# Block-causal attention feeding a feed-forward on one Trainium2 core: another order of a pair's eight steps from batch 2 on

## The chip, the cores and the metric

The kernel runs on one core of a Trainium2 chip. The metric is device time in microseconds, the median of several executions; less is better. Five engines work side by side, each through a queue of its own: TensorE (PE, with its weight loads PEld), VectorE (DVE), ScalarE (ACT), GpSimd (POOL), and SyncE (SP), which issues every DMA of this kernel.

## The reference

Attention in 8 batches of 8 heads, 576 positions, 64 elements a head; a position sees its own block of 64 positions and all earlier blocks. The heads' outputs, side by side, are the 4608 x 512 input of a feed-forward of width 2048.

```
scores = q @ k.T / sqrt(64)
scores = where(pos_i // 64 >= pos_j // 64, scores, -1e9)
attn   = exp(scores - max) / (sum + 1e-9)
x      = (attn @ v), heads side by side         # 4608 x 512
h      = x @ w_in                               # 4608 x 2048
g      = 0 where h <= -1, h where h >= 1, else (h + 1)^2 / 4
out    = g @ w_out                              # 4608 x 512
```

## The kernel before, in words

**Pairs and steps.** The work goes by pairs of heads: 8 batches of 4 pairs, 32 in all. `attention_steps` is a generator that emits a pair's attention in eight steps, each ended by a `yield` (L688, L699, L711, L722, L733, L742, L750, L759). From the 36th step on (`START`, L830) the main loop puts one half of a feed-forward tile behind each step: `ffn_in` (12 matmuls of 512 columns into the bank `ph`, then ScalarE `t`, two VectorE operations L780 and L783, ScalarE `gh`, GpSimd `gl`) or `ffn_out` (12 matmuls into `po`, for the tile before the last). In the pairs spoken of here, `ffn_out` stands behind steps 1, 3, 5 and 7, and `ffn_in` behind 2, 4, 6 and 8. What is left of the feed-forward runs alone at the end.

**Three kinds of pairs.** Pairs of batches 0 and 1 run in ways of their own. From batch 2 on (`FAR`, `RAW` = 2) a pair is "far": each operand is split into a high and a low part in float32r; a pair's last transpositions and its products with v reach into the next pair's steps. `cur` is the pair whose scores are made, `old` the one before, `nxt` the one after.

**What a far pair does.** For each head j there are three groups of query tiles (`GROUPS`, L258 on): group 0 (score tiles of 128 and 256 columns), group 1 (384) and group 2 (512); the last 64-position blocks of both heads make one further group, "last".
- `scores(j, g)` (L494): two matmuls a tile into a work bank; VectorE maximum (L505); ScalarE exponential with its sum (L509); VectorE adds the epsilon (L491), inverts (L492) and scales (L515) `pr`. Then a DMA copies `pr` to a float32r tile `prr` (`as_float32r`, L230, issued at L250). `scores_last` (L518) does this in two banks of 288 columns.
- `turn(j, g)` (L556): three or four transpositions of `prr` into a work bank (L552); ScalarE casts the high part (L545), VectorE subtracts it for the low part (L547). Group 0 goes to `pa`, groups 1 and 2 to `pb`. `turn_last` (L572) does four for `pb` in one bank and then a fifth, the 64 x 128 corner, for `pcs` in a bank of its own.
- `attn_v_first` (L631): the first 256 queries of both heads, 8 matmuls into one bank; `attn_v(j)` (L640): the other 320 queries of one head, 10 matmuls into a bank. `add_halves` (L608) then copies half of the bank to `xtmp` on ScalarE (L613) and adds the other half on VectorE into `x32` (L614). `xtmp` has one buffer, and each call allocates it anew.
- `store_x` (L647): ScalarE casts `x32` to `xh`, GpSimd subtracts for `xl`, the inputs of `ffn_in`.
- `turned_raw(j)` (L397) and `turned_last` (L437): transposition of the next keys and queries (four for head j, or one for both heads' last blocks) into a work bank, read four times or more by ScalarE and VectorE in turn (L388, L389, L394, L395; the last blocks also L446 twice).
- `begin` (L459) allocates `pa`, `pb` and `x32` anew and splits v.

**The work banks.** Behind the 36th step every `work_bank` (L80) comes from a ring of three PSUM banks, in the order of the calls: a call takes the bank of the third call before it, and its first matmul waits until the last reader there is done. A far pair makes 22 calls.

**The order before.** Steps of a far pair, before its feed-forward half; the bank calls in brackets:
1. `old.turn(1,1)`, `cur.scores(0,0)`, load of v, `old.attn_v_first` [3]
2. `old.turn(1,2)`, `cur.scores(0,1)`, `cur.turned_last`, a fetch for a later pair [3]
3. `old.attn_v(1)`, `old.store_x`, `cur.scores(0,2)` [2]
4. `begin`, `turn(0,0)`, `scores_last`, load of the next q and k [3]
5. `turn(0,1)`, `scores(1,0)`, `nxt.turned_raw(0)` [3]
6. `turn(0,2)`, `scores(1,1)` [2]
7. `turn_last` (two banks), `scores(1,2)` [3]
8. `turn(1,0)`, `attn_v(0)`, `nxt.turned_raw(1)` [3]

The framework orders each engine's queue by the program's order and by what its own plan takes to be ready; TensorE's queue in the trace is the program's order, VectorE's and ScalarE's differ from it in places. SyncE's queue carries the copies of P, the loads of q, k, v, the copies within q and k, and `wo` (L787) for each feed-forward tile.

Of the kernel before, what the change touches and what calls it, by code (L numbers as in the profile page):

```python
# [23 lines left out]
def block_attn_then_ffn(  # L24
# [230 lines left out]
    class Pair:  # L255
# [238 lines left out]
        def scores(self, j, g):  # L494
            tiles = self.GROUPS[g]
            m = len(tiles)
            ps = work_bank("ps_s")
            pr = att3.tile([P, S], F32, tag="pr", name="pr")
            nm = small.tile([P, 2], F32, tag="nm", name="nm")
            sm = small.tile([P, 2], F32, tag="sm", name="sm")  # L500
            cols = [slice(at, at + (t + 1) * P) for t, at in tiles]
            for (t, _), cs in zip(tiles, cols):
                self.product(ps[:, cs], j, t * P, 0, (t + 1) * P, True, True)
            for i, cs in enumerate(cols):
                nc.vector.tensor_reduce(  # L505
                    out=nm[:, i : i + 1], in_=ps[:, cs], axis=AX.X, op=ALU.max, negate=True
                )
            for i, cs in enumerate(cols):
                nc.scalar.activation(  # L509
                    pr[:, cs], ps[:, cs], AF.Exp, bias=nm[:, i : i + 1], scale=1.0,  # L510
                    accum_out=sm[:, i : i + 1],
                )
            self.inverse(sm[:, :m])
            for i, cs in enumerate(cols):
                nc.vector.tensor_scalar_mul(pr[:, cs], pr[:, cs], sm[:, i : i + 1])  # L515
            self.pr[j, g] = as_float32r(pr[:, : cols[-1].stop], self.plain) if self.hop else [pr]

        def scores_last(self):  # L518

# [19 lines left out]
            nc.vector.tensor_tensor(out=sm[:, 2:3], in0=sm[:, 0:1], in1=sm[:, 1:2], op=ALU.add)  # L539
            self.inverse(sm[:, 2:3])  # L540
            nc.vector.tensor_scalar_mul(pr, pr, sm[:, 2:3])
            self.pr["last"] = as_float32r(pr, self.plain) if self.hop else [pr]

        def split(self, ps, hi, lo=None):
            nc.scalar.copy(hi, ps)  # L545
# [25 lines left out]

        def turn_last(self):  # L572
            pr = self.pr.pop("last")
# [7 lines left out]
            ps = work_bank("ps_t")  # L581
            self.transposed(ps[:BLK, :P], pr, SM, BLK)
            self.split(
                ps[:BLK, :P].rearrange("p (h c) -> p h c", h=2), *(x[:BLK] for x in self.pc)
            )
# [22 lines left out]
        def add_halves(self, ps, j, c0):  # L608
# [4 lines left out]
            nc.scalar.copy(xtmp[main, :n], ps[rest, :])  # L613
            nc.vector.tensor_tensor(  # L614
                out=self.x32[main, c0 : c0 + n], in0=ps[main, :], in1=xtmp[main, :n], op=ALU.add
            )
# [14 lines left out]
        def attn_v_first(self):  # L631
            if self.plain:
                return self.both(0, self.parts_first)
            ps = work_bank("ps_av")
            for j in range(2):
                self.weighted(ps[:, j * G0 : (j + 1) * G0], j, self.parts_first(j))
            for j in range(2):
                self.add_halves(ps[:, j * G0 : (j + 1) * G0], j, 0)

        def attn_v(self, j):  # L640
            if self.plain:
                return self.both(G0, self.parts) if j else None
            ps = work_bank("ps_av")[:, :G1]
            self.weighted(ps, j, self.parts(j))
            self.add_halves(ps, j, G0)

        def store_x(self):  # L647

# [14 lines left out]
    def attention_steps():  # L663
# [10 lines left out]
        for i, cur in enumerate(pairs + [None]):  # L674
            nxt = pairs[i + 1] if i + 1 < len(pairs) else None
            far = old is not None and old.far
            near = old is not None and not old.far
            if far:
                old.turn(1, 1)
            if cur:  # L680
                cur.scores(0, 0)
                cur.turned(False, 1)
                cur.load("v")
            if far:
                old.attn_v_first()
# [8 lines left out]
            if i + 2 < len(pairs):  # L694
                pairs[i + 2].fetch()
# [7 lines left out]
            if not cur:  # L703
                return
            if cur.far:
                cur.scores(0, 2)
            else:
                cur.begin()
                cur.scores(0, 2)
                cur.turn(0, 0)  # L710
            yield  # L711
            if cur.far:
                cur.begin()
                cur.turn(0, 0)
                cur.scores_last()
            else:
                cur.scores_last()
                cur.turn(0, 1)
            if nxt:
# [5 lines left out]
            if cur.far:  # L725
                cur.turn(0, 1)
                cur.scores(1, 0)
            else:
                cur.scores(1, 0)
                cur.turn(0, 2)  # L730
            if nxt:
                nxt.turned(True, 0)
            yield  # L733
            if cur.far:
                cur.turn(0, 2)
                cur.scores(1, 1)
            else:
                cur.scores(1, 1)
                cur.turn_last()
            if nxt:  # L740
                nxt.turned(False, 0)
            yield  # L742
            if cur.far:
                cur.turn_last()
                cur.scores(1, 2)
            else:
                cur.scores(1, 2)
                cur.attn_v(0)
                cur.turn(1, 0)
            yield  # L750
# [134 lines left out]
```

## Time and profile before

| | |
|---|---|
| median of 3 executions | 1266.43 us (1266.29 to 1266.98) |
| the profiled execution | 1269.69 us |
| its span, first to last instruction | 1267.9 us, 20253 instructions |
| mean granted TensorE clock over the span | 0.981 |
| 0 to 280 us: TensorE busy | 231.38 us, clock 0.92 |
| 1080 us to the end (feed-forward alone): TensorE busy | 182.79 of 187.90 us, clock 0.99 |

The page gives each engine's busy time and, per group of instructions, what ended the idle time before it. The profile's windows give the same sums for any stretch. The far pairs fill the stretch between the two of the table: the first `turned_last` of a far pair stands at 274.4 us, the last at 1047.2. The profiled execution is 3.3 us above the median. "Busy" of a matmul includes the time in which it overlaps with its neighbours, so in a dense stretch the start-to-start distance is shorter than a matmul's own duration.

### The profile page before, as it was taken

How to read it: one execution, taken by the hardware profiler on the slowest of the kernel's cores; microseconds unless marked ns; L12 is line 12 of the kernel's file. 1: busy time of each engine (PE TensorE's matmuls, PEld its weight loads, DVE VectorE, ACT ScalarE, POOL GpSimd, SP SyncE). 2: the span in 40 equal slices, each digit the busy share in tenths (PEclk: the TensorE clock that was granted, in tenths of full speed). 3: DMA queues.
4: the chain of work that ended last, by engine and by line, in shares of the span. 5: the costliest groups of instructions: out<-in, count | busy, mean ns of one | idle time of the engine just before them, and what ended most of it. 6: DMA issues, size and time to landing. Idle time of an engine off the chain costs nothing.

```text
span 1267.9 us, 20253 instructions
## 1 busy us (share of the span) xinstructions
PE 1200.1 (95%) x6280; PEld 998.8 (79%) x6280; DVE 887.0 (70%) x2188; ACT 703.2 (55%) x1827; POOL 394.6 (31%) x430
## 2 busy tenths in 40 slices
PE   5888889899999999999999999999999999999998
PEld 4666667678888888888888888888888888888886
DVE  8898877758777777777777777787777777322222
ACT  5787656646566655665656655566556555222222
POOL 3555655522222222222222222222222222222222
PEclk9888988999999999999999999999999999999999
DMA  5566666667888655555554655465556433422432
GB/s 158 167 176 215 203 228 197 217 198 237 260 273 266 215 162 158 154 175 163 156 162 145 187 157 152 138 189 153 160 154 190 137 128 118 132 87 98 133 100 100
DMA packets 185259, 215.43 MB, mean 170 GB/s; under 512 B 113840, under 2 KB 132272, under 8 KB 184384
## 3 DMA queue, kind: packets, MB, share of 16 engines
q1 hardware_dynamic: 185152, 214.14, 54.9%
q8 instruction: 50, 0.82, 0.3%
q14 instruction: 57, 0.47, 0.1%
HBM read 134.74 MB, written 31.98 MB: 131 GB/s over the span
## 4 chain that ended last, share of the span: by engine, by line
PE 69%; DVE 16%; ACT 6%; issue 5%; DMA 1%; POOL 1%; SPq 1%; ACTq 0%; POOLq 0%; DVEq 0%
PE ph L770 29%; PE po L794 15%; PE po L799 7%; PE ps_av L591 7%; PE ps_s L482 4%; ACT pr L509 3%; PE ps_s L485 3%; DVE t L780 2%; PE ps_t L552 2%; DVE t L783 2%; ACT t L779 2%; DVE pb L547 2%; DVE nm L505 2%; DVE sm L491 1%; DVE pr L515 1%
## 5 line engine op out<-in xcount | busy, mean ns | idle before, releaser
L785 POOL TENSOR_TENSOR gl<-t,gh 128x512 fp32r<-128x512 f32 x144 | 187.5, 1302 | 510.2 <-ACT gh L784 333.2
L794 PE MATMUL po<-wo,gh 128*128 128x512 f32 x1152 | 296.1, 397 | 0.5 <-DMA wo<-wo_split 0.3
L794 PEld LDWEIGHTS po<-wo,gh 128*128 128x128 f32 x1152 | 212.5, 189 | 44.5 <-DMA wo<-wo_split 0.7
L770 PE MATMUL ph<-xh,wih 128*128 128x512 f32 x576 | 232.9, 404 | 1.6 <-DVE t L783 1.6
L770 PE MATMUL ph<-xh,wil 128*128 128x512 f32 x576 | 228.8, 397 | 0.0
L770 PE MATMUL ph<-xl,wih 128*128 128x512 f32 x576 | 227.8, 396 | 0.5 <-DVE xl L627 0.5
L780 DVE SCALAR_TENSOR_TENSOR t<-t 128x512 f32<-128x512 f32 x144 | 101.5, 705 | 168.0 <-ACT t L779 165.2
L779 ACT ACTIVATE t<-ph 128x512 f32<-128x512 f32 x144 | 85.9, 597 | 173.8 <-PE ph L770 173.8
L509 ACT ACTIVATE pr<-ps_s,nm 128x128 f32<-128x128 f32 (+3 forms) x256 | 134.1, 527 | 60.5 <-DVE nm L505 58.4
L784 ACT CAST gh<-t 128x512 fp32r<-128x512 f32 x144 | 89.5, 621 | 120.3 <-DVE t L783 120.0
L799 PE MATMUL po<-wo,gl 128*128 128x512 f32 x576 | 155.6, 392 | 0.0
L482 PE MATMUL ps_s<-ka,qa 68*128 68x288 f32 (+4 forms) x384 | 135.3, 367 | 15.0 <-ACT pr L509 5.4
L379 POOL TENSOR_TENSOR vsr<-vn,vsr 128x256 fp32r<-128x256 f32 (+1 forms) x96 | 55.2, 576 | 246.2 <-ACT vsr L378 244.6
L770 PEld LDWEIGHTS ph<-xh,wil 128*128 128x128 f32 x576 | 109.5, 190 | 23.8
L770 PEld LDWEIGHTS ph<-xh,wih 128*128 128x128 f32 x576 | 109.8, 191 | 21.7 <-DVE t L783 2.3
L799 PEld LDWEIGHTS po<-wo,gl 128*128 128x128 f32 x576 | 108.7, 189 | 23.1
L505 DVE TENSOR_REDUCE nm<-ps_s 128x1 f32<-128x128 f32 (+3 forms) x256 | 118.8, 482 | 10.4 <-PE ps_s L485 9.4
L770 PEld LDWEIGHTS ph<-xl,wih 128*128 128x128 f32 x576 | 109.7, 190 | 20.5 <-DVE xl L627 0.9
L485 PE MATMUL ps_s<-kb,qb 128*128 128x288 f32 (+4 forms) x384 | 121.1, 322 | 0.0
L515 DVE TENSOR_SCALAR pr<-pr,sm 128x128 f32<-128x128 f32 (+3 forms) x256 | 107.3, 440 | 5.4
L783 DVE TENSOR_TENSOR t<-ph,t 128x512 f32<-128x512 f32 x144 | 98.7, 686 | 2.2
L491 DVE TENSOR_SCALAR sm<-sm 128x1 f32<-128x1 f32 (+1 forms) x224 | 52.0, 232 | 68.3 <-ACT pr L509 65.7
(111 smaller groups left out, 1871.4 us busy)
## 6 DMA issues: line engine op xcount, KB each, us to landing
wo<-wo_split SPq DMA_DIRECT2D x144, 512.0 KB, 3.5
prr<-pr SPq DMA_DIRECT2D x96, 192.0 KB, 2.5
prr<-pr SPq DMA_DIRECT2D x72, 256.0 KB, 2.8
out_dram<-ob SPq DMA_DIRECT2D x36, 256.0 KB, 2.9
bits<-in_moe_w_in_dram SPq DMA_DIRECT2D x32, 256.0 KB, 3.5
bits<-in_moe_w_out_dram SPq DMA_DIRECT2D x32, 256.0 KB, 3.0
wo_split<-ws SPq DMA_DIRECT2D x16, 512.0 KB, 2.9
qa<-qb SPq DMA_DIRECT2D x63, 128.0 KB, 2.4
```

The costliest lines, as they stand in the source:

```text
L482: nc.tensor.matmul(ps, qa[:KA, j, c0 : c0 + P], ka[:KA, j, k0 : k0 + n], start=first, stop=False)
L485: nc.tensor.matmul(ps, qb[:, j, c0 : c0 + P], kb[:, j, k0 : k0 + n], start=False, stop=last)
L505: nc.vector.tensor_reduce(out=nm[:, i : i + 1], in_=ps[:, cs], axis=AX.X, op=ALU.max, negate=True)
L509: nc.scalar.activation(pr[:, cs], ps[:, cs], AF.Exp, bias=nm[:, i : i + 1], scale=1.0, accum_out=sm[:, i : i + 1],)
L515: nc.vector.tensor_scalar_mul(pr[:, cs], pr[:, cs], sm[:, i : i + 1])
L770: nc.tensor.matmul(ph, w[:, cc, fs], x[:, cc, xs], start=(cc == 0 and i == 0), stop=(cc == NCC - 1 and i == 2),)
L779: nc.scalar.activation(t_, ph, AF.Relu, bias=0.5, scale=0.5)
L780: nc.vector.scalar_tensor_tensor(out=t_, in0=t_, scalar=1.0, in1=t_, op0=ALU.min, op1=ALU.mult)
L783: nc.vector.tensor_tensor(out=t_, in0=ph, in1=t_, op=ALU.max)
L785: nc.gpsimd.tensor_tensor(out=gl, in0=t_, in1=gh.bitcast(F32), op=ALU.subtract)
L794: nc.tensor.matmul(po[tt], gh[:, ts_], wo[:, w, :], start=(fc == 0 and w == 0), stop=False)
L799: nc.tensor.matmul(po[tt], gl[:, ts_], wo[:, 0, :], start=False, stop=fc == NFC - 1)
```

## The change

It concerns far pairs only, and one line of the pair before the first of them. What each step does after:
1. `cur.scores(0,0)`, load of v, `old.attn_v(0)`, `old.turn(1,1)`, copy of P [3]
2. `cur.scores(0,1)`, fetch, `old.turn(1,2)`, `old.attn_v_first`, copy of P [3]
3. `cur.scores(0,2)`, `old.attn_v(1)`, `old.store_x`, copy of P [2]
4. `begin`, `scores_last`, `turn(0,0)`, copy of P, load of the next q and k [3]
5. `scores(1,0)`, `turn(0,1)`, copy of P, `nxt.turned_raw(0)` [3]
6. `scores(1,1)`, `turn(0,2)`, copy of P [2]
7. `scores(1,2)`, `turn_last` (one bank), `nxt.turned_raw(1)`, copy of P [3]
8. `turn(1,0)` with the corner in the free 128 columns of its bank, `nxt.turned_last` [2]

So scores stand first in every step; the DMA copy of P (`move`) is issued after the step's transpositions; the corner goes to step 8; head 0's products with v go from step 8 to step 1 of the next pair, the first parts from step 1 to step 2; `turned_raw(1)` goes from step 8 to step 7 and `turned_last` from step 2 to step 8 of the pair before. `attn_v_first` allocates `xtmp` once for both heads, which use different rows of it. The diff, cut to its core:

```diff
-            self.pr[j, g] = as_float32r(pr[:, : cols[-1].stop], self.plain) if self.hop else [pr]
+            self.pr[j, g] = [pr[:, : cols[-1].stop]]
+            if not self.far:
+                self.moved(j, g)
+
+        def moved(self, *key):
+            if self.hop:
+                self.pr[key] = as_float32r(self.pr[key][0], self.plain)
+
+        def move(self, *key):
+            if self.far:
+                self.moved(*key)
...
             for c0 in range(0, n, P):
                 self.transposed(ps[:, c0 : c0 + P], pr, c0, P)
+            if self.far and j == 1 and g == 0:
+                self.turn_corner(self.pr.pop(("last",)), ps[:BLK, n : n + P])
...
+        def turn_corner(self, pr, ps):
+            self.transposed(ps, pr, SM, BLK)
+            self.split(ps.rearrange("p (h c) -> p h c", h=2), *(x[:BLK] for x in self.pc))
...
-            xtmp = att1.tile([P, G1], F32, tag="xtmp", name="xtmp")
             nc.scalar.copy(xtmp[main, :n], ps[rest, :])
...
+            xtmp = att1.tile([P, G1], F32, tag="xtmp", name="xtmp")
             for j in range(2):
-                self.add_halves(ps[:, j * G0 : (j + 1) * G0], j, 0)
+                self.add_halves(ps[:, j * G0 : (j + 1) * G0], j, 0, xtmp)
...
-            if far:
-                old.turn(1, 1)
             if cur:
                 cur.scores(0, 0)
                 cur.turned(False, 1)
                 cur.load("v")
             if far:
-                old.attn_v_first()
+                old.attn_v(0)
+                old.turn(1, 1)
...
+            if cur:
+                cur.move(0, 0)
             yield
+            if cur:
+                cur.scores(0, 1)
+                if not cur.raw:
+                    cur.turned_last()
+            if i + 2 < len(pairs):
+                pairs[i + 2].fetch()
             if far:
                 old.turn(1, 2)
-            if cur:
-                cur.scores(0, 1)
-                cur.turned_last()
...
+                old.attn_v_first()
...
+            if cur:
+                cur.move(0, 1)
             yield
             if far:
+                if cur:
+                    cur.scores(0, 2)
                 old.attn_v(1)
                 old.store_x()
...
             if cur.far:
                 cur.begin()
+                cur.scores_last()
                 cur.turn(0, 0)
-                cur.scores_last()
...
+            cur.scores(1, 0)
+            cur.turn(0, 1 if cur.far else 2)
+            cur.move(1, 0)
...
+            cur.scores(1, 1)
             if cur.far:
                 cur.turn(0, 2)
-                cur.scores(1, 1)
...
+            cur.scores(1, 2)
             if cur.far:
                 cur.turn_last()
-                cur.scores(1, 2)
+                if nxt:
+                    nxt.turned(True, 1)
...
             if cur.far:
                 cur.turn(1, 0)
-                cur.attn_v(0)
...
-            if nxt:
+            if nxt and not cur.far:
                 nxt.turned(True, 1)
+            if nxt and nxt.raw:
+                nxt.turned_last()
             yield
```

More of the change, by code (lines that the diff above doesn't have):

```diff
@@ L541, in scores_last @@
             nc.vector.tensor_scalar_mul(pr, pr, sm[:, 2:3])
-            self.pr["last"] = as_float32r(pr, self.plain) if self.hop else [pr]
+            self.pr["last",] = [pr]
+            if not self.far:
+                self.moved("last")
         def split(self, ps, hi, lo=None):
@@ L572, in turn_last @@
         def turn_last(self):
-            pr = self.pr.pop("last")
+            pr = self.pr["last",] if self.far else self.pr.pop(("last",))
             ps = work_bank("ps_t")
@@ L580, in turn_last @@
             )
[L581 to L585, printed above, removed]
+            if not self.far:
+                self.turn_corner(pr, work_bank("ps_t")[:BLK, :P])
+        def turn_corner(self, pr, ps):
+            self.transposed(ps, pr, SM, BLK)
+            self.split(ps.rearrange("p (h c) -> p h c", h=2), *(x[:BLK] for x in self.pc))
         def weighted(self, ps, j, parts, first=True, last=True):
@@ L644, in attn_v @@
             self.weighted(ps, j, self.parts(j))
-            self.add_halves(ps, j, G0)
+            self.add_halves(ps, j, G0, att1.tile([P, G1], F32, tag="xtmp", name="xtmp"))
         def store_x(self):
@@ L710, in attention_steps @@
                 cur.turn(0, 0)
+            cur.move(0, 2)
             yield
@@ L718, in attention_steps @@
                 cur.turn(0, 1)
+            cur.move("last")
             if nxt:
@@ L733, in attention_steps @@
             yield
+            cur.scores(1, 1)
             if cur.far:
                 cur.turn(0, 2)
-                cur.scores(1, 1)
             else:
-                cur.scores(1, 1)
                 cur.turn_last()
+            cur.move(1, 1)
             if nxt:
@@ L742, in attention_steps @@
             yield
+            cur.scores(1, 2)
             if cur.far:
                 cur.turn_last()
-                cur.scores(1, 2)
+                if nxt:
+                    nxt.turned(True, 1)
             else:
-                cur.scores(1, 2)
                 cur.attn_v(0)
                 cur.turn(1, 0)
+            cur.move(1, 2)
             yield
```

19 lines of the change are left out of this document (7 added, 12 removed).

## The prediction

> **What bounds the kernel now.** I read the stages first, with a window for each. The change touches only the pairs from batch 2 on, and these lie in the middle stage. Columns: stretch, its length, busy time and count for five engines, granted clock, DMA share, GB/s.
>
> ```profile
> 280.00:1080.00 800.00, 785.88 (x4353) 665.98 (x4353) 613.70 (x1506) 477.01 (x1227) 210.46 (x219) 1.00 0.58 175
> ```
>
> TensorE is busy 98% of this stage at full clock, VectorE 77%, ScalarE 60%. TensorE sets the end, and only what it loses can be won. Second, the waits in this stage, on the matmul track and on the weight-load track.
>
> ```profile
> PE ps_qk L442 <- DVE x L614: 8.9, 23, 0.4
> PE ps_s L482 <- ACT pr L509: 5.2, 17, 0.3
> PEld ps_qk L442 <- PE ps_s L485: 15.7, 23, 0.7
> PEld ps_s L482 <- ACT pr L509: 10.1, 23, 0.5
> ```
>
> Two places repeat once a pair: the transposition of the next keys' and queries' last blocks (L442, step 2), and the 512-column scores of head 1 (L482, step 7). Both wait for one of the three work banks. The timeline of one pair shows their size.
>
> ```profile
> 611.83 0.34 PE L485 MATMUL ps_s<-kb,qb 128*128 128x384 f32 x1
> 612.55 0.25 PE L442 MATMUL ps_qk<-ident_r,qk 128*128 128x128 f32 x1 [0.38 <-DVE x L614]
> ...
> 631.54 0.51 PE L552 MATMUL ps_t<-ident_r,prr 128*128 128x128 f32 x5
> 632.35 0.50 PE L482 MATMUL ps_s<-ka,qa 68*128 68x512 f32 x1 [0.30 <-ACT pr L509]
> ...
> 632.92 2.00 PE L794 MATMUL po<-wo,gh 128*128 128x512 f32 x8
> 634.76 1.07 PE L799 MATMUL po<-wo,gl 128*128 128x512 f32 x4
> ```
>
> Matmuls overlap, so I count from start to start. Eight of 512 columns start in 634.76 - 632.92 = 1.84 us, 0.23 each, so 384 columns need 0.17; L442 came 0.72 after L485: 0.55 lost. The chain of waits has the five transpositions in step 7:
>
> ```profile
> 631.70 0.36 PE ps_t L552 x5
> ```
>
> That is 0.072 each; L482 came 0.81 after the first: 0.45 lost.
>
> **The change part by part.** *What it removes.* First place: the bank is that of the first attention parts, and its last reader is late.
>
> ```profile
> 608.73 0.37 ACT L613 COPY xtmp<-ps_av 64x256 f32<-64x256 f32 x1
> ...
> 611.25 0.37 ACT L613 COPY xtmp<-ps_av 64x256 f32<-64x256 f32 x1
> ...
> 610.08 0.41 DVE L614 TENSOR_TENSOR x<-ps_av,xtmp 64x256 f32<-64x256 f32 x1
> ...
> 611.98 0.43 DVE L614 TENSOR_TENSOR x<-ps_av,xtmp 64x256 f32<-64x256 f32 x1
> ```
>
> Head 1's copy runs 2.5 us behind head 0's: `xtmp` is one buffer, so it waits for head 0's add (610.08 to 610.49) and then falls behind the exponentials. After the change both heads share one allocation with rows of their own, the last-block transposition has moved a step and more away (end of step 8), and the bank of the first parts is next taken in step 4, with all of step 3 between. This wait has no place left: 23 x 0.55 = 12.6 us.
>
> Second place: step 7 asks for the bank of head 1's 384-column scores.
>
> ```profile
> 630.43 0.69 DVE L547 TENSOR_TENSOR pb<-ps_t,pb 128x512 fp32r<-128x512 f32 x1
> 631.04 0.55 DVE L505 TENSOR_REDUCE nm<-ps_s 128x1 f32<-128x384 f32 x1
> ...
> 632.10 0.19 ACT L509 ACTIVATION_READ_ACCUMULATOR pr<-ps_s,nm 128x1 f32 x1
> ```
>
> The bank comes free at 632.10 + 0.19 = 632.29; TensorE wanted it at 631.54 + 0.36 = 631.90. After, scores stand ahead of transpositions, so the maximum (631.04) no longer stands behind the subtraction (630.43): free at about 632.29 - 0.61 = 631.68. The corner's own bank is gone, so step 7's scores take the bank of step 5's last transpositions, and head 1's old 384-column bank is asked for second, at 631.54 + (632.92 - 632.35) = 632.11: a margin of 0.4 us. By the weight-load row this place is worth 10.1 us.
>
> Together 12.6 + 10.1 = 22.7 us. The matmul track's idle alone gives 8.9 + 5.2 = 14.1 us, the weight-load track's 15.7 + 10.1 = 25.8; these are the ends I keep. I take start to start, because it needs neither a matmul's end nor a load that would have idled anyway. The Trainium skill, Perfetto Trace Analysis, section Tensor Engine Instruction (MATMUL, LD_WEIGHTS), marks the profiled end of a matmul as estimated; by that rule the weight-load figure is the better one, and the time would be near 1240.6 us. In this trace the 0.34 us of the L485 row for 0.17 us of streaming agrees that an end is no measure of occupancy.
>
> *What it adds and moves.* No operation is added on any engine: same transpositions, casts, subtractions, DMAs. One bank a pair is saved (21 for 22). What changes is where the work falls, so I balance VectorE against TensorE by step, 1 to 8 of one pair:
>
> ```profile
> 606.87:611.29 4.42, 4.42 (x29) 3.87 (x27) 2.97 (x8) 3.32 (x10) 1.60 (x2) 1.00 0.13 30
> 611.29:615.48 4.19, 3.81 (x20) 3.00 (x19) 3.90 (x12) 2.12 (x6) 0.43 (x1) 1.00 0.61 192
> 615.48:620.02 4.54, 4.54 (x25) 3.91 (x24) 3.88 (x10) 3.43 (x8) 2.18 (x3) 1.00 0.48 124
> 620.02:624.14 4.12, 4.12 (x24) 3.56 (x23) 2.08 (x8) 1.55 (x5) 1.72 (x2) 1.00 0.74 200
> 624.14:628.00 3.86, 3.86 (x24) 3.31 (x23) 3.46 (x7) 2.74 (x7) 0.42 (x1) 1.00 0.73 220
> 628.00:631.54 3.54, 3.54 (x20) 2.98 (x18) 3.14 (x8) 1.44 (x4) 0.87 (x1) 1.00 0.60 192
> 631.54:635.67 4.13, 3.83 (x20) 3.05 (x19) 3.32 (x9) 2.40 (x6) 0.00 (x0) 1.00 0.29 90
> 635.67:640.40 4.73, 4.73 (x31) 4.16 (x30) 2.91 (x8) 2.89 (x7) 1.61 (x2) 1.00 0.62 199
> ```
>
> ```profile
> 607.08 0.29 PE L482 MATMUL ps_s<-ka,qa 68*128 68x128 f32 x1
> ...
> 607.61 1.03 PE L591 MATMUL ps_av<-pa,vsr 128*128 128x256 f32 x8
> ...
> 636.04 1.31 PE ps_av L591 x10
> ...
> L389 DVE SCALAR_TENSOR_TENSOR qb<-ps_qk,qb 64x128 fp32r<-64x128 f32 x24 | 6.8, 284 | 0.8
> L614 DVE TENSOR_TENSOR x<-ps_av,xtmp 64x320 f32<-64x320 f32 x48 | 23.4, 488 | 0.8
> ```
>
> TensorE in steps 4 to 8: 4.12 + 3.86 + 3.54 as before; step 7 is 4.13 - 0.45 (the wait) - 0.07 (corner) + 0.29 (four transpositions from step 8) = 3.90; step 8 is 4.73 - 1.31 (head 0's parts, to step 1) - 0.29 + 0.14 (corner, last blocks) = 3.27. Sum 18.69 against 20.38. VectorE there: 2.08 + 3.46 + 3.14 + 3.32 + 2.91 = 14.91, less head 0's add 0.49, plus four last-block reads of 0.284 = 1.14: 15.56. To that come round trips to ScalarE that VectorE can't fill:
>
> ```profile
> DVE sm L491 <- ACT pr L509: 60.7, 99, 1.0
> DVE sm L539 <- ACT pr L535: 27.4, 24, 1.1
> DVE t L780 <- ACT t L779: 24.6, 52, 0.7
> DVE pa L547 <- ACT pa L545: 21.3, 30, 0.8
> DVE kb L395 <- ACT kb L394: 14.9, 23, 0.7
> ```
>
> Three softmaxes of 60.7/99 = 0.61, the last row's 27.4/24 = 1.14 and the keys' 14.9/23 = 0.65 make 3.6; so 19.2 us of VectorE stand beside 18.69 us of TensorE. VectorE, at rest in step 4, falls some 0.5 us further behind by the end of step 8. TensorE runs on as long as a bank's readers are done within about a step: in the new order a bank is asked for again 3.3 us or more after its last matmul (the shortest is step 8's, since that step is 3.27 long). Today's two waits ended at 612.41, 3.8 us after the first parts (607.61 + 1.03), and at 632.29, over 3.2 us after scores that were done within 1 us of step 6's start at 628.00. So the new order lives with margins of half a microsecond, not with ease. In steps 1 to 3 TensorE has the parts of both heads, and VectorE catches up.
>
> The copies of P (`move`) now come last in their step, on SyncE's queue behind the v load and the fetch, ahead of `wo`. That queue already stands up to 4.4 us for P:
>
> ```profile
> SPq L250 <- DVE pr L515: 142.5, 99, 4.4
> ```
>
> P is wanted three steps later, with two whole steps between, at the least 3.54 + 3.90 = 7.4 us, so I cost this at nothing; without that cover TensorE's transpositions would wait. The copy of x in step 3 comes 0.57 us later (scores first); feed-forward reads it a step behind and, for the pair just finished, in its last three matmuls: nothing.
>
> New waits: bounded by nothing and by the 0.45 us a pair of the nearest row (10 us in all); a gain excludes itself, as no work is removed. I take 0.1 us a pair, 2.3 us, since the margins are positive but small.
>
> Sum: 1269.7 us of the profiled execution - 22.7 + 2.3 = 1249.3. That execution stands 3.3 us above the median of 1266.4, so by the median 1246.0.
>
> **The rivals.** *Partly given back.* VectorE's order may be less kind than my walk, and a new bank wait of 0.3 to 0.7 us a pair appears in steps 7, 8 or 1: 23 x 0.3 to 23 x 0.7 is 7 to 16 us, so 1251 to 1260. For it: margins of half a microsecond. Against: each margin is wider than the one it replaces.
>
> *No change.* VectorE already sets the pair's period, and TensorE's wait only moves on. For it: 25.7 us busy and some 4.5 of round trips (60.7 + 27.4 + 14.9 over 23) in a pair of 33.5. Against: in this stage VectorE itself waits for TensorE's data (through ScalarE's `t` and `pa`) 24.6 + 21.3 = 45.9 us, 2.0 a pair, twice what TensorE is to win. It would give 1266.
>
> *Slower.* Step 8 is the shortest, and its feed-forward matmuls end just as the four last-block reads are due.
>
> ```profile
> 633.05 0.69 DVE L780 SCALAR_TENSOR_TENSOR t<-t 128x512 f32<-128x512 f32 x1
> ...
> 632.67 0.59 ACT L545 CAST pb<-ps_t 128x512 fp32r<-128x512 f32 x1
> ```
>
> If VectorE's queue holds feed-forward's two operations (0.69 each, after 24.6/52 = 0.47 for ScalarE) ahead of these reads, the bank is free 0.47 + 1.38 + 1.14 = 2.99 us after step 8; step 1 wants it for head 1's transpositions after scores (607.61 - 607.08 = 0.53) and parts (1.31), at 1.84. TensorE would stand 1.15 us a pair, 26 us, more than the 22.7 won: 1270. It decides once the readers leave 1.0 us too late. Against: at 633.05 L780 went ahead of the last blocks' subtraction, but that one's own cast (632.67 + 0.59) was not done. The Trainium skill, PSUM — Partial Sum Buffer, section Engine vs sequencer instructions, calls these queues strict FIFO; by that rule a ready read couldn't pass L780, and the time would be this rival's if the order is so. No row here shows the new order.
>
> **How the numbers follow.** Forecast 0.61, partly given back 0.18, no change 0.09, slower 0.12. Some 0.2% (2.5 us) is what a measurement here can tell from no change. Faster is 0.61 + 0.18 = 0.79, same 0.09, slower 0.12. The likeliest time is 1246.0; its own range runs from 1241 (weight-load bound) to 1251. The range that holds 8 in 10 takes in the first rival: 1241 to 1262.
>
> **What would show it.** Right: no L442 or L482 row among TensorE's waits in the stage, a period near 32.6 instead of 33.5, head 1's `xtmp` copy right behind head 0's, VectorE's waits for ScalarE's `t` shorter. The first step is wrong if L442 still waits for L614; the second if L482 or L552 of step 7 waits for L509. A wait of L552 or L591 in step 1 for a last-block read speaks for the slower rival. My forecast is wrong if TensorE's idle in this stage stays above 10 us, or VectorE's lag at the end of step 8 exceeds a step.

## The result and the profile after

The changed kernel takes 1280.42 us (median of 4, 1277.82 to 1281.73) against 1266.7 us for the kernel before (1266.29 to 1268.13): a ratio of 1.0091, 95% interval 1.0073 to 1.0109. It is slower, by some 13.7 us; the forecast was 1246. The profiled execution took 1279.28 us, its span 1277.5 us.

TensorE's waits in the stage of the far pairs (280 to 1080 us), first on the matmul track, then on the weight-load track:

```profile
PE ps_av L608 <- DVE pb L560: 10.6, 23, 0.5
PE ps_t L565 <- DVE x L630: 4.6, 23, 0.2
PE ps_av L608 <- DVE pa L560: 2.1, 13, 0.2
...
PEld ps_av L608 <- DVE pb L560: 13.9, 23, 0.6
PEld ps_t L565 <- DVE x L630: 12.1, 23, 0.6
PEld ps_av L608 <- PE ps_s L485: 7.5, 23, 0.3
```

(L608, L565, L630 and L560 are L591, L552, L614 and L547 of the kernel before.) The two waits of before, L442 and L482, have no row any more. In their place TensorE waits once in step 1 and twice in step 2. The timeline of one pair:

```profile
608.41 0.28 PE L485 MATMUL ps_s<-kb,qb 128*128 128x256 f32 x1
608.81 1.32 PE L608 MATMUL ps_av<-pb,vsr 128*128 128x320 f32 x8
...
613.41 0.34 PE L485 MATMUL ps_s<-kb,qb 128*128 128x384 f32 x1
613.98 0.54 PE L565 MATMUL ps_t<-ident_r,prr 128*128 128x128 f32 x4 [0.22 <-DVE x L630]
614.97 1.14 PE L608 MATMUL ps_av<-pa,vsr 128*128 128x256 f32 x8 [0.46 <-DVE pb L560]
```

From start to start, less 0.12 us for 256 columns, 0.17 for 384 and 0.29 for four transpositions: 0.28 + 0.40 + 0.70 = 1.38 us lost a pair, against 0.55 + 0.45 = 1.00 before. The 0.38 us more come to 8.7 us over 23 pairs. The chain that ended last says who holds TensorE up; the line of before, then that of after:

```profile
PE 69%; DVE 16%; ACT 6%; issue 5%; DMA 1%; POOL 1%; SPq 1%; ACTq 0%; POOLq 0%; DVEq 0%
```

```profile
PE 47%; DVE 34%; ACT 6%; issue 5%; DMA 3%; POOL 2%; SPq 1%; ACTq 0%; POOLq 0%; DVEq 0%
```

VectorE's share has doubled. Its busy time in the stage (third of the five engines) rose from 613.70 us to this, for as many operations:

```profile
280.00:1080.00 800.00, 778.98 (x4289) 660.55 (x4288) 652.97 (x1497) 476.81 (x1219) 211.96 (x218) 1.00 0.58 173
```

VectorE's groups by shape in that stage show which operations became longer (busy time, mean ns of one); before, and after:

```profile
L515 DVE TENSOR_SCALAR pr<-pr,sm 128x512 f32<-128x512 f32 x48 | 23.7, 493 | 1.7
L491 DVE TENSOR_SCALAR sm<-sm 128x2 f32<-128x2 f32 x47 | 23.4, 497 | 23.3 <-ACT pr L509 23.3
L515 DVE TENSOR_SCALAR pr<-pr,sm 128x384 f32<-128x384 f32 x47 | 19.7, 420 | 1.4
...
L533 DVE TENSOR_TENSOR nm<-nm 128x1 f32<-128x1 f32 x24 | 3.8, 159 | 0.8
```

```profile
L515 DVE TENSOR_SCALAR pr<-pr,sm 128x512 f32<-128x512 f32 x48 | 40.5, 844 | 1.6
L515 DVE TENSOR_SCALAR pr<-pr,sm 128x384 f32<-128x384 f32 x47 | 30.7, 653 | 1.9 <-DVE sm L492 0.3
L491 DVE TENSOR_SCALAR sm<-sm 128x2 f32<-128x2 f32 x47 | 27.4, 582 | 28.3 <-ACT pr L509 27.6
...
L544 DVE TENSOR_TENSOR nm<-nm 128x1 f32<-128x1 f32 x24 | 13.5, 563 | 0.8
```

That is 16.8 + 11.0 + 4.0 + 9.7 = 41.5 us more in four groups, with shapes and counts unchanged. The timeline shows the longest case, the scaling of head 1's 512 columns at the border of steps 7 and 8, beside GpSimd:

```profile
638.94 1.36 DVE L515 TENSOR_SCALAR pr<-pr,sm 128x512 f32<-128x512 f32 x1
```

```profile
638.72 1.29 POOL L814 TENSOR_TENSOR gl<-t,gh 128x512 fp32r<-128x512 f32 x1 [6.85 <-ACT gh L813]
```

The scaling begins 0.22 us after `gl` and ends 0.29 us after it: 1.36 us for work that takes 0.49 elsewhere. No row of the waits names this, since the instruction counts as busy while it is held. The Trainium skill, SBUF — State Buffer, section Who interferes with whom, says that VectorE's two-port modes, which `tensor_scalar` can enter, and its instructions with two SBUF inputs share a port pair with GpSimd under an exclusive lock, so that whichever starts second is held until the other is done. The three durations above agree with it, and the one-column `nm` (two SBUF inputs; 159 to 563 ns, beside `xl`) does too. So does the other direction: the `gl` that starts at 622.45 us, 0.08 us into a scaling of 0.48, takes 1.56 us instead of 1.29.

A measure for the stage alone, free of the 290 us ahead of it: the starts of ScalarE's cast of x (`store_x`) for the first and the last far pair, 23 pairs apart. Before, and after:

```profile
L656 ACT CAST xh<-x x32: 350/578/677, 318.4 to 1083.7; 128x576 fp32r<-128x576 f32 x16, 128x384 fp32r<-128x384 f32 x8, 128x192 fp32r<-128x192 f32 x8
```

```profile
L673 ACT CAST xh<-x x32: 346/596/682, 317.1 to 1093.2; 128x576 fp32r<-128x576 f32 x16, 128x384 fp32r<-128x384 f32 x8, 128x192 fp32r<-128x192 f32 x8
```

The distance grew from 765.3 to 776.1 us, by 10.8. It is called the far distance below; each comes from one profiled execution. The kernel before and the one with one `xtmp`, whose waits are the same, differ by 0.2 us in it.

### The profile page after: what moved, and what is told of

It is laid out like the page before. It is cut to its first block, busy times and chain, and to the rows that moved or that the text cites. A ratio compares the mean times of both kernels' runs of the same rounds, so it can differ in the third digit from the quotient of the medians.

```text
span 1277.5 us, 20236 instructions
## 1 busy us (share of the span) xinstructions
PE 1201.2 (94%) x6280; PEld 1001.4 (78%) x6280; DVE 931.9 (73%) x2188; ACT 707.6 (55%) x1827; POOL 398.1 (31%) x430
## 4 chain that ended last, share of the span: by engine, by line
PE 47%; DVE 34%; ACT 6%; issue 5%; DMA 3%; POOL 2%; SPq 1%; ACTq 0%; POOLq 0%; DVEq 0%
PE ph L799 19%; PE po L823 10%; PE ps_av L608 6%; DVE pr L515 5%; PE po L828 5%; DVE nm L505 4%; DVE t L809 3%; DVE pb L560 3%; DVE t L812 3%; DVE kb L395 3%; DVE sm L491 2%; ACT pr L509 2%; PE ps_s L482 2%; PE ps_s L485 2%; DVE qb L389 2%
## 5 line engine op out<-in xcount | busy, mean ns | idle before, releaser
L814 POOL TENSOR_TENSOR gl<-t,gh 128x512 fp32r<-128x512 f32 x144 | 192.9, 1340 | 604.7 <-ACT gh L813 426.6
L823 PEld LDWEIGHTS po<-wo,gh 128*128 128x128 f32 x1152 | 208.6, 189 | 41.9 <-DMA wo<-wo_split 2.4
L799 PE MATMUL ph<-xh,wih 128*128 128x512 f32 x576 | 235.9, 409 | 2.1 <-DVE t L812 2.1
L505 DVE TENSOR_REDUCE nm<-ps_s 128x1 f32<-128x128 f32 (+3 forms) x256 | 123.3, 484 | 29.9 <-PE ps_s L485 28.4
L515 DVE TENSOR_SCALAR pr<-pr,sm 128x128 f32<-128x128 f32 (+3 forms) x256 | 135.0, 548 | 5.1 <-DVE sm L492 0.3
L482 PE MATMUL ps_s<-ka,qa 68*128 68x288 f32 (+4 forms) x384 | 123.3, 336 | 8.5 <-ACT kb L427 2.9
L482 PEld LDWEIGHTS ps_s<-ka,qa 68*128 68x128 f32 x384 | 75.0, 195 | 18.8 <-ACT kb L427 3.6
```

Source lines behind the costliest of these rows:

```text
L482: nc.tensor.matmul(ps, qa[:KA, j, c0 : c0 + P], ka[:KA, j, k0 : k0 + n], start=first, stop=False)
L505: nc.vector.tensor_reduce(out=nm[:, i : i + 1], in_=ps[:, cs], axis=AX.X, op=ALU.max, negate=True)
L799: nc.tensor.matmul(ph, w[:, cc, fs], x[:, cc, xs], start=(cc == 0 and i == 0), stop=(cc == NCC - 1 and i == 2),)
L814: nc.gpsimd.tensor_tensor(out=gl, in0=t_, in1=gh.bitcast(F32), op=ALU.subtract)
L823: nc.tensor.matmul(po[tt], gh[:, ts_], wo[:, w, :], start=(fc == 0 and w == 0), stop=False)
```

## The experiments

Three theories. A: VectorE is late because operations of its own now fall beside GpSimd's subtractions and are held. B: VectorE is late because of the work that was moved, above all the four last-block reads that came into step 8. C: TensorE's waits have another cause than VectorE's lateness, or VectorE's load sets the pair's period whatever is done. Each ratio is against the kernel before on the same chip.

| kernel | median us | ratio, 95% interval | far distance us |
|---|---|---|---|
| before | 1266.7 | | 765.3 |
| changed | 1280.42 | 1.0091, 1.0073 to 1.0109 | 776.1 |
| changed, short gl (part of the low-order correction left out) | 1253.63 | 0.9884, 0.986 to 0.9909 | 753.9 |
| before, short gl (the same left out) | 1247.52 | 0.9846, 0.9827 to 0.9866 | 751.4 |
| changed, gl in halves | 1277.26 | 1.0073, 1.0058 to 1.0088 | 772.3 |
| changed, 512-column scaling on ScalarE | 1267.76 | 1.0003, 0.9989 to 1.0017 | 764.7 |
| changed, last blocks back in step 2 | 1265.32 | 0.998, 0.9969 to 0.999 | 763.2 |
| both of these | 1267.17 | 0.9989, 0.9977 to 1.0001 | 762.9 |
| before, last blocks in step 8 | 1282.26 | 1.011, 1.0083 to 1.0137 | 779.5 |
| changed, step 1 transpositions first | 1270.69 | 1.0016, 0.9997 to 1.0034 | 767.9 |
| before, one xtmp | 1266.84 | 0.9988, 0.9974 to 1.0002 | 765.1 |
| the same, step 7 scores first | 1262.94 | 0.996, 0.9945 to 0.9975 | 759.3 |
| the same, all far scalings on ScalarE | 1270.41 | 1.0021, 1.0012 to 1.0031 | 767.2 |
| before, no addition | 1266.74 | 0.9993, 0.9972 to 1.0014 | 760.3 |
| changed, no addition | 1268.9 | 1.0003, 0.9986 to 1.002 | 760.8 |
| before, one xtmp, step 7 scores first, no addition | 1265.08 | 0.9979, 0.9962 to 0.9996 | 758.3 |
| changed, 512 on ScalarE, no addition in far pairs | 1256.19 | 0.99, 0.9883 to 0.9917 | 753.1 |
| the same, last blocks back in step 2 | 1258.84 | 0.9919, 0.9902 to 0.9935 | 754.7 |
| before, 512 on ScalarE, no addition in far pairs | 1264.86 | 0.9979, 0.9962 to 0.9995 | 761.1 |
| the same, one xtmp, step 7 scores first | 1262.21 | 0.9952, 0.9935 to 0.9969 | 758.8 |

### GpSimd's subtraction made short, in both orders

```diff
-        nc.gpsimd.tensor_tensor(out=gl, in0=t_, in1=gh.bitcast(F32), op=ALU.subtract)
+        nc.gpsimd.tensor_tensor(
+            out=gl[:, :P], in0=t_[:, :P], in1=gh[:, :P].bitcast(F32), op=ALU.subtract
+        )
...
-            nc.tensor.matmul(po[tt], gl[:, ts_], wo[:, 0, :], start=False, stop=fc == NFC - 1)
+            nc.tensor.matmul(po[tt], gl[:, :P], wo[:, 0, :], start=False, stop=fc == NFC - 1)
```

> The changed kernel with GpSimd's subtraction gl made on 128 of its 512 columns (the feed-forward's third products read those 128 for all four tiles, so part of the low-order correction is left out); VectorE's queue in the far pairs is the same as in the changed kernel. Theory A, that VectorE is held up by GpSimd's subtractions which the new order puts beside it: the 512-column scaling L515 falls from a mean of 0.86 us to 0.49, TensorE's waits in step 2 (4.6 + 10.6 us on the matmul track) fall by half or more, and the time falls by 10 to 22 us, to 1258 to 1270. Theory B, that the moved work alone (last blocks in step 8, head 1's transpositions in step 7) makes VectorE late: scalings shorten but the time stays within 4 us of 1280.

> The kernel before with the same quarter-width gl (the same part of the low-order correction is left out), as the control. Theory A: little of VectorE's time is lost to gl here except in the two-column L491 (13 us over its shortest), so the time falls by 0 to 6 us, clearly less than in the changed kernel. Theory B: the same fall in both kernels.

VectorE's groups in the stage, changed kernel with short gl:

```profile
L515 DVE TENSOR_SCALAR pr<-pr,sm 128x512 f32<-128x512 f32 x48 | 24.0, 499 | 1.6
L491 DVE TENSOR_SCALAR sm<-sm 128x2 f32<-128x2 f32 x47 | 8.0, 169 | 28.3 <-ACT pr L509 27.6
```

The scaling is back at 499 ns, and the two-column addition is at 169, which shows that it was held in the old order too (497). The changed kernel's far distance falls by 22.2 us and its time to 1253.63, below the range that A gave, and what is left of step 2's waits is this:

```profile
PE ps_av L608 <- DVE pb L560: 6.5, 23, 0.4
```

But the control fell too, to 1247.52 and by 13.9 us of far distance, where A had said 0 to 6 us of time: gl held VectorE in the old order as well, by way of L491. TensorE's two old waits, 8.9 and 5.2 us, went with it, up to this one:

```profile
PE ps_qk L442 <- DVE x L614: 0.3, 1, 0.3
```

So the cost of standing beside gl is shown. The difference between the orders shrinks from 10.8 to 2.5 us of far distance when gl is short, and from 13.7 to 6.1 us in the medians, which hold the first 290 us too; the old order stays the faster one. That the old order was free of the holding is refuted, and so is B's equal fall in both.

### The same subtraction in two halves

```diff
+        for h0 in range(0, TCH, TCH // 2):
+            hs = slice(h0, h0 + TCH // 2)
...
```

> The changed kernel with gl made in two GpSimd instructions of 256 columns, full work, VectorE's queue unchanged. Theory A: a scaling that comes upon gl waits for one half at most, about 0.65 us instead of 1.3; the mean of the 512-column L515 falls from 0.86 to 0.6 or 0.75 and the time falls by 4 to 12 us. Theory B: no change, within 3 us of 1280; or a little slower through GpSimd's second fixed cost.

```profile
L491 DVE TENSOR_SCALAR sm<-sm 128x2 f32<-128x2 f32 x47 | 34.2, 727 | 28.3 <-ACT pr L509 27.6
L515 DVE TENSOR_SCALAR pr<-pr,sm 128x512 f32<-128x512 f32 x48 | 31.9, 665 | 1.6
```

The 512-column scaling falls as A said (844 to 665 ns), but the two-column addition rises (582 to 727). The net is 3.2 us of time, below the 4 to 12 that A gave and inside B's 3 us of 1280: this run does not separate the two.

### One suspect at a time, in the new order

The 512-column scaling on ScalarE, which leaves the rest of VectorE's queue as it was:

```diff
-                nc.vector.tensor_scalar_mul(pr[:, cs], pr[:, cs], sm[:, i : i + 1])
+                if self.far and g == 2:
+                    nc.scalar.mul(pr[:, cs], pr[:, cs], sm[:, i : i + 1])
+                else:
+                    nc.vector.tensor_scalar_mul(pr[:, cs], pr[:, cs], sm[:, i : i + 1])
```

> The changed kernel with the scaling of the 512-column groups (L515, far pairs) on ScalarE; the rest of VectorE's queue is unchanged. Theory A (VectorE blocked by GpSimd's gl in that scaling): 39 us of VectorE time go, 17 of them blocking, TensorE's waits in step 2 shrink by more than half, and the time falls by 12 to 25 us, to 1255 to 1268. Theory B (the moved work): VectorE is relieved of 0.49 us in a step that is not the one that is late, and the time falls by less than 5 us.

The last blocks' transposition back in step 2 of the pair that uses it, behind the first parts:

```diff
+            if late:
+                cur.turned_last()
...
-            if nxt and nxt.raw:
-                nxt.turned_last()
```

> The changed kernel with the last blocks' transposition back in step 2 of the pair that uses them, the rest as changed. Theory B (VectorE is late because those four reads came into step 8): waits of step 1 and 2 go, 1262 to 1270. Theory A: the 1.36 us scaling stays beside gl and the time stays within 6 us of 1280, with a new wait at L442.

Both at once:

> The changed kernel with both reliefs at once: the last blocks' transposition back in step 2 of the pair that uses it, and the 512-column scalings on ScalarE; VectorE's queue is otherwise that of the kernel with the last blocks back. Alone each took some 13 us off the changed kernel. If the two are separate costs (0.87 us beside gl, 1.14 us of reads, one after the other on VectorE) they add in part: 1252 to 1262. If they are one lateness that either relief takes away, nothing more comes: 1263 to 1268.

Each alone takes the far distance back to that of before or just below (764.7, 763.2). In time, A's reading of the first run and B's reading of the second came true (1267.76, 1265.32), where only one theory was to be right; both reliefs together bring no more (762.9). What they take away is one lateness, and either is enough. Being held is not enough for it: with the last blocks back in step 2 the scaling is held as long as in the changed kernel, and the other three groups stand at 657, 592 and 562 ns.

```profile
L515 DVE TENSOR_SCALAR pr<-pr,sm 128x512 f32<-128x512 f32 x48 | 40.4, 842 | 1.6
```

What stays in each of the three is the largest wait, that of the first parts in step 2 (10.6 us with either relief, as in the changed kernel), though A had said that step 2's waits would shrink by more than half and B that they would go; with both:

```profile
PE ps_av L611 <- DVE pb L563: 10.1, 22, 0.5
```

### One part of the change alone, in the old order

```diff
                 cur.scores(0, 1)
-                cur.turned_last()
+                if not cur.raw:
+                    cur.turned_last()
...
+            if nxt and nxt.raw:
+                nxt.turned_last()
             yield
```

> The kernel before with one part of the change alone: the last blocks' transposition at the end of step 8 of the pair before. This takes away the bank wait of L442 as the prediction had it. If its 12.6 us are won and step 8, which still holds head 0's parts, bears the four reads: 1252 to 1258. If the four reads make VectorE late for step 1 and 2: a new wait there and 1262 to 1275.

1282 us, as slow as the whole change. TensorE's waits in the stage:

```profile
PE ps_av L591 <- DVE ka L446: 8.4, 23, 0.6
PE ps_s L482 <- ACT pr L509: 5.3, 17, 0.4
PE ps_qk L442 <- DVE pa L547: 5.2, 17, 0.5
```

The old wait of step 7 stays, L442 now waits for another bank, and in step 1 the first parts wait for the last-block reads. VectorE's queue there:

```profile
612.38 0.69 DVE L783 SCALAR_TENSOR_TENSOR t<-t 128x512 f32<-128x512 f32 x1 [0.90 <-ACT t L782]
613.11 0.29 DVE L395 TENSOR_TENSOR kb<-ps_qk,kb 64x128 fp32r<-64x128 f32 x1
613.41 0.28 DVE L446 TENSOR_SCALAR qa<-ps_qk 64x128 fp32r<-64x128 f32 x1
613.71 0.29 DVE L446 TENSOR_SCALAR ka<-ps_qk 64x128 fp32r<-64x128 f32 x1
```

Feed-forward's operation (L783 here) stands ahead of three of the four reads, and waits 0.90 us for ScalarE first. This is the mechanism of the prediction's slower rival, in the place it named. No group of VectorE's is held more here than in the kernel before (487 ns for the 512-column scaling, 485 for the two-column addition). In the old order the reads in step 8 are enough by themselves to lose what the change lost.

### Step 1's transpositions first again

> The changed kernel with step 1's transpositions ahead of the scores again (head 0's parts stay behind them). On VectorE the subtraction for head 1's second group then stands ahead of the softmax of the pair's first scores instead of behind its round trip to ScalarE. If the 10.6 us wait of the first parts in step 2 comes from that place in the queue: it goes, 6 to 12 us less than 1280, 1268 to 1274. If it comes from VectorE's lateness alone, it stays, or moves to the bank of the scores: within 4 us of 1280.

```profile
PE ps_s L482 <- PE ps_t L565: 6.9, 22, 0.3
PE ps_av L608 <- DVE ka L446: 6.0, 22, 0.3
```

The first parts' wait goes and the median falls by 9.7 us, as expected of a place in the queue; but a wait for the last-block reads comes up in step 1. Moving the wait ahead in time makes it smaller, not gone.

### The prediction's first step alone: one xtmp

> The kernel before with one xtmp for both heads in the first attention parts, and nothing else. If the bank wait of L442 is what the prediction priced, it goes: 12 us less, about 1254. If VectorE's own load sets the pair's period (theory C), the wait moves to another place and the time stays within 3 us of 1266.

Nothing: the far distance is 765.1 and L442's row is as before. ScalarE's two copies in this kernel:

```profile
606.02 0.37 ACT L612 COPY xtmp<-ps_av 64x256 f32<-64x256 f32 x1
...
608.54 0.37 ACT L612 COPY xtmp<-ps_av 64x256 f32<-64x256 f32 x1
```

Still 2.5 us apart, and the changed kernel has the same wait:

```profile
617.78 0.37 ACT L629 COPY xtmp<-ps_av 64x256 f32<-64x256 f32 x1 [1.00 <-DVE x L630]
```

So `xtmp` was not what parted them. Copy and add read one PSUM bank; that the framework keeps the two engines apart there is the likely reason, argued and not tried.

With step 7's scores ahead of the last blocks, nothing else moved:

> The same, and in step 7 the scores ahead of the last blocks' transpositions. If both waits were priced rightly and nothing takes their place: 20 to 23 us less than before, about 1244 to 1247. Theory C: within 3 us of 1266.

The time, 1262.94 us, lies between the two ranges given. L482's wait is gone and L442's stays (9.3 us on the matmul track): 6.0 us of far distance for a place that was priced at 10.1. The 512-column scaling rises from 493 to 619 ns there, so VectorE may have given back a part.

And with every far scaling on ScalarE:

> The kernel before, with scores ahead of the last blocks in step 7 and every scaling of the far pairs on ScalarE: 3.6 us a pair off VectorE, some 4.8 us a pair onto ScalarE (20 of 33.5 busy now). If VectorE's lateness is what TensorE waits for, in the old order too: both waits go and the time is 1240 to 1250. If ScalarE becomes late in its place (its exponentials behind the scalings): 1262 or more.

1270: ScalarE becomes late in its place, as the second reading had it; VectorE waits 54.1 us in the stage for ScalarE's casts of `pa`, against 21.8 without this edit. Relief for VectorE has to be chosen, not maximal.

### The addition of 1e-9 left out

```diff
-            nc.vector.tensor_scalar_add(total, total, EPS)
```

> The kernel before without the addition of 1e-9 to the softmax sums (L491, seven a pair on VectorE; the sums are at least 1 after the maximum is taken off, so float32 keeps the same value). In the far pairs L491 costs VectorE 41 us, 13 of them spent beside gl in the two-column form just ahead of the bank that L442 waits for. If VectorE's lateness is what TensorE waits for in the old order (theory A): L442's 8.9 us go, the time falls by 10 to 20 us, to 1248 to 1258. If TensorE's waits have another cause (theory C): within 4 us of 1268.

> The changed kernel without the same addition. Theory A: some 44 us of VectorE go, but the 512-column scaling still stands beside gl; the waits of step 2 shrink and the time falls by 10 to 20 us, to 1260 to 1270, and stays above the old order without the addition. Theory C: within 4 us of 1280.

> The kernel before with scores ahead of the last blocks in step 7 and without the addition: both of TensorE's waits aimed at, no work moved between steps. Theory A: 16 to 24 us less than before, 1244 to 1252, the fastest so far with all its work. If the freed VectorE only brings another scaling beside gl: 1254 to 1262.

The changed kernel's far distance falls by 15.3 us, the old order's by 5.0: with VectorE relieved the orders are level (760.8 and 760.3). The first parts' wait has no row any more in the changed kernel, although the 512-column scaling is held longer than ever there (940 ns). In time, the changed kernel is where A had put it (1268.9); the old order did not move (1266.74, as C had it), and with step 7's scores first it is above both ranges (1265.08). In the old order L442's wait even grows, from 8.9 to 11.8 us, against A.

Without the addition the framework puts head 1's add behind two scalings, so the bank that L442 needs comes no sooner. The medians show less than the far distance: the far pairs of these three kernels begin 3 to 8 us later than without the edit, and TensorE's granted clock over the first 290 us was 0.89, 0.90 and 0.89, where the other 17 profiles have 0.91 to 0.94. Why it was lower isn't shown.

### Room for VectorE, in both orders

The 512-column scaling on ScalarE and no addition in the far pairs:

> The changed kernel with the 512-column scalings on ScalarE and without the addition in the far pairs, the last blocks left in step 8. If reads of the last blocks no longer matter once VectorE has room: within 4 us of the run that has them in step 2. If they still make VectorE late: 5 to 12 us above it.

> The same without the addition of 1e-9 to the sums in the far pairs (the sums are at least 1, so float32 keeps the value): VectorE has 2.5 us a pair less than in the changed kernel. If lateness of VectorE is all that TensorE waits for in the new order: the first parts' wait (10.6 us) goes too, 1243 to 1254. If the wait of the first parts is fixed by its place in the queue: 1256 to 1264.

> The kernel before with the same two reliefs as the fastest run so far (512-column scalings on ScalarE, no addition of 1e-9 in the far pairs). If the new order is worth something once VectorE has room, the old order with the reliefs keeps a bank wait at L442 and stays at 1259 to 1266, above the new order's 1256. If the reliefs did all of it: 1250 to 1257.

> The same with scores ahead of the last blocks in step 7. One bank wait fewer than the run beside it if L482's wait is still there: 2 to 6 us below it; else the same time.

The new order is then the fastest kernel of this study among those that leave out no more than the addition: 1256.19 us, ratio 0.99. TensorE is busy 795.61 of the stage's 800 us, and its only row among the matmul waits is this:

```profile
PE ps_t L569 <- DVE x L634: 3.2, 15, 0.3
```

The last blocks in step 8 cost nothing now (753.1 against 754.7 with them in step 2), and the first parts' wait is gone from both, so it was lateness and not only a place in the queue; 1258.84 us for the second lies in the range that stood for a fixed place, but the rows decide that. The old order with the same reliefs keeps its wait at L442 and stays at 1264.86, or 1262.21 with step 7 turned round:

```profile
PE ps_qk L442 <- DVE x L618: 11.7, 23, 0.8
```

So with these two reliefs the new order is worth some 6 to 9 us, and 6 to 8 us of far distance. That does not hold for every relief: with gl short the old order was 2.5 us of far distance ahead (751.4 against 753.9).

## Why the prediction was wrong

**What bounds the kernel.** Half right. TensorE is never far from full, but the prediction read VectorE's 77% as room. In the chain of after VectorE, with short pieces of ScalarE between, holds from step 5 to step 2 (628.3 to 648.7 us, of a period of 33.8), and in the old order too TensorE's lost time was VectorE's lateness: short gl alone took both waits away there and gave back 13.9 us of far distance.

**What it removes.** The two waits did go in the changed kernel, as forecast. Of the reasons given for the first, one `xtmp` does nothing by itself; moving the transposition away does it (in the old order with the last blocks in step 8, L442 waits for `pa` and no longer for `x`). The second, removed alone, was worth 6.0 us, not 10.1.

**What it adds and moves: the step that failed.** "No operation is added on any engine", and so each duration was taken from its old place. VectorE's balance for steps 4 to 8 (15.56 us busy and 3.6 of round trips, 19.2 beside 18.69) put the growth of its lag at half a microsecond. The durations depend on the place: the 512-column scaling came to stand beside gl and took 1.36 us instead of 0.49, which is 0.87 us on VectorE's path in the very step that was shortest; two-column additions, 384-column scalings and the minimum of step 4 grew as well, 41.5 us in the stage. The window from VectorE's first work in step 4 to the end of the last-block reads shows the sum (VectorE is the third engine):

```profile
624.03:643.36 19.33, 19.17 (x108) 16.30 (x107) 17.28 (x39) 11.82 (x29) 4.23 (x4) 1.00 0.65 193
```

It is busy 17.28 us in it, 1.7 more than the balance had. That the length, 19.3, is near the forecast's 19.2 is luck: being late, VectorE waits for ScalarE 1.3 us there instead of 3.6. TensorE needs 18.5 us for the same steps (623.29 to 641.80). The reads end at 643.36 (643.07 + 0.29 below), while step 1 has begun at 641.80:

```profile
641.80 0.22 PE L482 MATMUL ps_s<-ka,qa 68*128 68x128 f32 x1
```

```profile
643.07 0.29 DVE L446 TENSOR_SCALAR ka<-ps_qk 64x128 fp32r<-64x128 f32 x1
643.40 0.69 DVE L809 SCALAR_TENSOR_TENSOR t<-t 128x512 f32<-128x512 f32 x1
```

That is 1.6 us late with feed-forward's operations still to come, so the softmax of step 1, its subtraction for `pb` and the banks of step 2 are late in turn. The margins of half a microsecond were gone before the round trip of step 1 began.

The second half of the step is "In steps 1 to 3 ... VectorE catches up", which has no sum behind it. Of the 1.38 us a pair, 0.70 are lost there, by the first parts in step 2. With the scores first in step 1, the subtraction for `pb` stands behind the softmax, and so behind VectorE's wait for its exponentials:

```profile
612.74 0.60 DVE L491 TENSOR_SCALAR sm<-sm 128x2 f32<-128x2 f32 x1 [1.17 <-ACT pr L509]
...
614.38 0.54 DVE L560 TENSOR_TENSOR pb<-ps_t,pb 128x384 fp32r<-128x384 f32 x1
```

Neither relief of step 8 touches this wait; it goes with step 1's transpositions first or without the addition.

**The new waits.** "I take 0.1 us a pair": measured 1.38. The upper bound of 0.45, from the nearest row, was too low by a factor of three. Two of the signs of being right came true in a slower kernel, since L442 and L482 have no row and VectorE's waits for ScalarE's `t` fell from 27.1 to 10.1 us; the period was 33.7 us (776.1 over 23), not 32.6.

**The rivals.** The slower one had the side and the step right: reads in step 8 leave VectorE late for step 1. It came in pure form only when the reads were moved alone. In the changed kernel the queue holds the reads ahead of feed-forward (643.07 before 643.40 above), and the wait falls mostly in step 2; it was given 0.12, and 1270 was still 10 us short. "No change" had argued from 25.7 us busy and 4.5 of round trips; the argument against it was VectorE's room, 45.9 us of waits for TensorE's data. That room was there and was used up: in the stage its waits for `t` and `pa` fell from 27.1 + 21.3 to 10.1 + 5.3 us, 33 in all, while its busy time grew by 39.3.

**What stays open.** How much of the changed kernel's loss is held time and how much moved work can't be divided: either relief alone ends the loss, though the whole held time stays in one of them. The held time of the 384-column scalings beside `vsr` and of the minimum beside `xl` was not taken away by itself. Nor was the corner's move: in the bank that it now shares, ScalarE's cast of `pa` waits for VectorE's `pcs` (34.0 us in the stage). With the last blocks back this wait stays (37.9 us) and the loss is gone, so it is not enough by itself; what it adds isn't known.

## What to carry to other kernels

Before moving work of an engine to another place, list what the engine that shares its memory ports runs there: a duration read in one place is not the duration in another, and no row of waits will tell. VectorE, busy 82% of the changed kernel's stage, was the bound for some 60% of a period; balance by step, with held time and round trips, and ask for a margin larger than the sum of the unknowns. When a bank wait is moved by reordering, first give the engine that empties the banks less to do; here the order paid only then, and not with every relief.

## What the runs showed of the hardware

A 128x512 scaling from SBUF to SBUF takes 0.49 us alone and 1.36 when it starts 0.22 us into GpSimd's 1.29 us subtraction; that subtraction takes 1.56 us when it starts 0.08 us into the scaling. A two-column addition takes 169 ns with GpSimd's instruction at a quarter, and 582 beside the full one, 727 beside two halves. Where the addition was left out in all pairs, TensorE's granted clock over the first 290 us was 0.89 or 0.90, in one profile of each kernel, and 0.91 to 0.94 elsewhere; the cause isn't shown.
